# Where the causal mask of an attention unit is set: a product on TensorE, or a select on GpSimd

## The chip, the cores and the metric

One NeuronCore of a Trainium2 chip runs the whole program. The metric is device time in microseconds (us). The engines are called PE (TensorE; PEld is its weight load, which overlaps), DVE (VectorE), ACT (ScalarE), POOL (GpSimd) and SP (SyncE, which issues DMAs). Each works through its own queue in order.

## What is computed

The reference runs a gated linear attention (an mLSTM) over 2 batches, 8 heads, 768 positions and 40 values per head, and feeds its output through two gated feed-forward blocks over 1536 tokens, 320 wide, with 1536 hidden columns.

```python
for t in range(S):
    m_new  = max(f[t] + m, i[t])
    C = exp(f[t] + m - m_new) * C + exp(i[t] - m_new) * outer(v[t], k[t])
    n = exp(f[t] + m - m_new) * n + exp(i[t] - m_new) * k[t]
    y[t] = sigmoid(o[t]) * (C @ q[t]) / max(abs(n . q[t]), 1)
x = silu(xn @ w_gate) * (xn @ w_val) @ w_out        # xn: y, rms-normed
z = sigmoid(x @ w2_gate) * (x @ w2_val) @ w2_out
```

The kernel does not step through t. It cuts the 768 positions into six chunks of 128. Inside a chunk every position s acts on every later t with the weight exp(u[t] + a[s]) times the score k[s].q[t], and nothing acts on an earlier t: that is the causal mask. What came before the chunk is in a state matrix.

## The kernel before

**Units.** A unit is one chunk of one batch: unit u holds chunk u // 2 of batch u % 2, so there are twelve, and units 4 to 11 are chunks two to five (counted from zero). For a unit, `a_bcast_pe` (L270) builds the exponents in two PSUM tiles `A`, each 128 x 512 (s on the partitions, four heads of 128 values of t along a row). Per half it takes: one product of the bf16 identity with `negm` (L259, in `a_bcast0`), which writes 0 where t >= s and -1e30 elsewhere; one product with `picked` (L275), which adds one gate term; and four narrow products (L278), which add the other. `a_exp` (L300) has ACT take the exponential of each half into the SBUF tile `E` (L304), so a masked place becomes 0. `a_scores` (L309) computes the scores into PSUM, eight products per unit and half pair (L317); `a_weigh` (L320) has DVE multiply each half of `E` by its scores in place (L324). `a_out` (L326) uses `E` as weights of the output product (L337), after the product with the state (L333). Normalisation, gating, transposing and splitting follow. `A` and the scores share the two PSUM buffers of tag `sc`; `E` has two SBUF buffers.

**Feed-forward.** `steps` is a list of (block, token group, hidden tile) slots. A slot runs sixteen products into PSUM (`up`, L454), the activation on ACT and DVE (L483 to L486 for the first block), a subtraction on POOL that makes the low part of the hidden tile (L487), and two slots later the down products (L465 to L467). Weights arrive as 544 KB pieces in `wraw` (three buffers, L96) and go through ACT (L100, L107, L120) and DVE (L111, L124) to become a high and a low part. The first token groups run while later attention units are still being computed, so PE has both in one queue.

**What sets the order.** The work of units 0 and 1 is written out by hand. From unit 3 on, each operation has a due time (`want`, L562): a unit starts a set lead ahead of the slot that needs it, its stages stand 1.5 us apart (`stg`), and a planner that estimates each operation places all of them in the queues of the engines. So the queues before are a plan's result, and a changed operation can move others in it. In a unit, the first stage holds `a_scale`, `a_bcast_pe` and `a_exp`, the second `a_scores`, `a_wv` and `a_gate`, the third `a_weigh`, the fourth `a_out`.

**What else POOL does** in that stretch: L487 (hT), L287 (`wv`), L349 (state decay), L407 (`r`), L413 (a copy of `y`).

Of the kernel before, what the change touches and what calls it, by code (L numbers as in the profile page):

```python
# [12 lines left out]
AF = mybir.ActivationFunctionType  # L13
ALU = mybir.AluOpType
# [5 lines left out]
L = 128  # L20
# [22 lines left out]


PE_ADD = 6

G2 = [(0, 2), (2, 4), (6, 4), (10, 2)]
T = dict(
    visits=[(0, 0, 12), (1, 0, 12), (2, 0, 12), (3, 0, 12)],
    start=9.89, d0=4.6, d1=2.84, d2=5.36, w0=1.9, w1=-11.36, wld=9.1, lead=(33, 35, 35, 35, 42, 60), skew=3.0, stg=1.5,  # L50
# [6 lines left out]
def attention_then_two_moe(tc, fi, fir, qk, qt3, nat, w1, w2, rms_g, consts, out):  # L57
    nc = tc.nc
# [9 lines left out]
    def psum(tag):  # L68
        return ps.tile([128, 512], F32, tag=tag, name=tag, bufs=2)
# [9 lines left out]
    rows3 = [ap.tile([KR, 3, L], BF16, name=f"rows3_{b}", bufs=1) for b in range(B)]  # L79
# [150 lines left out]
    def col(u, k):  # L230
        c, b = divmod(u, B)
        if c == 0:
            return col0[:, k * BH + b * H:k * BH + (b + 1) * H]
        o = b * H * NR + c - 1
        return colR[:, o:o + (H - 1) * NR + 1:NR]
# [18 lines left out]
    def a_bcast0(u, tag="up"):  # L254
        d = X.setdefault(u, {})
        d["E"] = ap.tile([128, H, L], F32, tag="E", name="E")
        d["A"] = [psum(tag) for _ in range(2)]
        for hh in range(2):
            nc.tensor.matmul(d["A"][hh], lhsT=identb, rhs=negm.unsqueeze(1).to_broadcast([128, 4, L]), start=True, stop=False)  # L259

    def a_bcast0b(u, hh):
# [5 lines left out]
    def picked(r, n, m):  # L267
        return pick[:, r:r + (n - 1) * NR + 1:NR].unsqueeze(2).to_broadcast([KR, n, m])

    def a_bcast_pe(u):  # L270
        c, b = divmod(u, B)
        a_bcast0(u, "sc")
        for hh in range(2):
            o, r = X[u]["A"][hh], hh * 4 * NR + c - 1
            nc.tensor.matmul(o, lhsT=rows3[b][:, 1], rhs=picked(r, 4, L), start=False, stop=False)  # L275
            for h in range(4):
                one = pick[:, r + h * NR:r + h * NR + 1].to_broadcast([KR, L])
                nc.tensor.matmul(o[:, h * L:(h + 1) * L], lhsT=one, rhs=rows3[b][:, 0], start=False, stop=(h == 3))  # L278
# [21 lines left out]
    def a_exp(u, hs=range(H)):  # L300
        E, A = X[u]["E"], X[u]["A"]
        if u >= B:
            for hh in range(2):
                nc.scalar.activation(E[:, 4 * hh:4 * hh + 4, :].rearrange("p h t -> p (h t)"), A[hh], AF.Exp)  # L304
            return
        for h in hs:
            nc.scalar.activation(E[:, h, :], A[h // 4][:, h % 4 * L:(h % 4 + 1) * L], AF.Exp, bias=col(u, 0)[:, h:h + 1])
# [43 lines left out]
    def a_state(u):  # L351
# [6 lines left out]
        for g in range(NG):  # L358
            n = GW if g < 2 else 2 * E1
            o = s[0:KR, g * GW:g * GW + n]  # L360
            add = B <= u < PE_ADD
            nc.tensor.matmul(o, lhsT=d["nat"][:, g * KR:(g + 1) * KR], rhs=wv[:, g * GW:g * GW + n], start=True, stop=not add)
# [3 lines left out]
    def a_update(u):  # L366
# [4 lines left out]
        st = St[b].rearrange("p g e -> p (g e)")[:, 0:NV]  # L371
        if u < PE_ADD:
            nc.vector.tensor_tensor(out=st, in0=blk, in1=d["C"][0:KR, 0:NV], op=ALU.mult)
# [234 lines left out]
    def unit(u):  # L608
        t = t_unit(u) + (u % B) * T["skew"]
        st = [  # L610
            [a_scale, a_bcast_pe, a_exp] if u > B else [a_scale, a_exp],
            [a_scores, a_wv, a_gate],
            [a_weigh] if u < PE_ADD else [a_weigh, a_state],
            [a_out, a_decay, a_state, a_update] if u < PE_ADD else [a_out, a_decay, a_update],
            [a_norm1, a_norm1b, a_norm1c],
            [a_norm2],
            [a_norm3, a_flip],
            [a_xt],
        ]
        if u >= B:  # L620
            want(t - T["uld"], lambda: a_load(u))
        for k, fns in enumerate(st):
            want(t + k * T["stg"], *[lambda fn=fn: fn(u) for fn in fns])
# [7 lines left out]
    with tc.manual_schedule(engines=set(engines)):  # L631
# [6 lines left out]
        for t, fill in ((ident, 1.0), (identb, 1.0)):  # L638
            nc.gpsimd.memset(t, 0.0)
            nc.gpsimd.affine_select(out=t, in_=t, pattern=[[1, 128]], compare_op=ALU.not_equal,  # L640
                                    fill=fill, base=0, channel_multiplier=-1)
# [5 lines left out]
                                fill=NEG, base=0, channel_multiplier=-1)  # L647
        nc.gpsimd.memset(mhalf, -0.5)
        nc.gpsimd.memset(pick, 0.0)
        for k in range(3):  # L650
            nc.gpsimd.affine_select(out=pick, in_=pick, pattern=[[1, 9 * NR]], compare_op=ALU.not_equal,
                                    fill=1.0, base=k * H * NR, channel_multiplier=-1)
        nc.gpsimd.memset(blk9, 1.0)
        b4 = blk9.rearrange("p (g j e) -> p g j e", g=NG, j=3)
        for base, cm, st in ((0, 1, -D), (D - 1, -1, D)):
            nc.gpsimd.affine_select(out=b4, in_=b4, pattern=[[0, NG], [st, 3], [0, E1]], compare_op=ALU.is_ge,
                                    fill=0.0, base=base, channel_multiplier=cm)
# [10 lines left out]

        keep_warm(wm[0])
        a_bcast0(0)  # L670
        g_first()
        g_max()
# [14 lines left out]
        g_first_a()  # L687
        a_bcast0b(0, 1)
        a_exp(0)
        w_bits(0, 0, 0)  # L690
        a_load(1, (3,))
# [4 lines left out]
        w_hi(0, 0, 0)  # L696
        w_pre(0, 0, 1)
        a_bcast0(1)
        a_bcast0b(1, 0)
        a_bcast0b(1, 1)  # L700
        w_bits(0, 0, 1)
        g_first_ws()
        a_exp(1)
        keep_warm(wm[2])
        w_lo(0, 0, 0)
# [21 lines left out]
        a_norm1b(1)  # L727
        a_norm2(0)
        a_bcast_pe(2)
        a_norm1c(1)  # L730
        a_norm2(1)
# [38 lines left out]
    for s, (moe, g, m, f, l) in enumerate(steps):  # L770
# [6 lines left out]
        r = []  # L777
# [81 lines left out]
```

## Time and profile before

| | us |
|---|---|
| runs | 543.25, 538.78, 543.01 |
| median | 543.01 |
| profiled execution | 540.2 |
| span of its profile (first to last instruction) | 538.5 |
| mean granted clock of TensorE | 0.971 of full speed |

The profile lists busy time by engine, the chain of work that ended last, the costliest groups of instructions and the DMA queues. A busy PE is not PE at its peak, since matmuls are pipelined and their ends are modelled; the start of one matmul to the start of the next is what one costs the queue. The granted clock has two levels, 2.4 GHz (1.00) and 1.2 GHz (0.50); a figure between them is a stretch that holds some of both.

### The profile page before, as it was taken

The numbers are of one execution on the slowest core, as the hardware profiler recorded it, in microseconds if no ns is written. First come the engines' busy times: TensorE is split into PE (matmuls) and PEld (weight loads), VectorE is DVE, ScalarE is ACT, GpSimd is POOL, SyncE is SP. The second block draws the span as 40 slices with busy tenths as digits, with TensorE's granted clock in tenths as the row PEclk, the third lists the DMA queues.
The fourth block names the chain that finished last, engine by engine and source line by source line (L and its number), as shares of the span: only waits on it lengthen the run. The fifth ranks groups of instructions, "written<-read, shape, count | busy, mean of one in ns | idle before, by whom it ended". The sixth has DMA issues, their size and how long they took to land.

```text
span 538.5 us, 9054 instructions
## 1 busy us (share of the span) xinstructions
PE 518.2 (96%) x3592; PEld 478.5 (89%) x3592; DVE 260.1 (48%) x540; ACT 232.4 (43%) x518; POOL 95.2 (18%) x148
## 2 busy tenths in 40 slices
PE   7779999799999999999999999999999999999997
PEld 5668888799999988999999999998888888888996
DVE  5768879444243433654765756643233232323322
ACT  4669878533222322332757666643222222222222
POOL 7112233243223221222321212110000000000000
PEclk9888999799989997999999999999999999999999
DMA  6598878411021112100225333100000010000100
GB/s 187 177 287 271 265 240 257 169 53 40 1 77 53 40 47 71 54 1 1 84 85 167 116 134 120 48 0 13 13 0 2 0 42 8 1 0 1 50 1 25
DMA packets 15752, 43.09 MB, mean 80 GB/s; under 512 B 1822, under 2 KB 6734, under 8 KB 15710
## 3 DMA queue, kind: packets, MB, share of 16 engines
q1 hardware_dynamic: 15518, 42.27, 25.0%
q8 instruction: 28, 0.46, 0.4%
q10 hardware_dynamic: 192, 0.25, 0.1%
q14 instruction: 14, 0.11, 0.1%
HBM read 40.32 MB, written 2.01 MB: 79 GB/s over the span
## 4 chain that ended last, share of the span: by engine, by line
PE 67%; DMA 15%; ACT 8%; DVE 7%; issue 3%; SPq 0%; ACTq 0%; DVEq 0%
PE up L454 29%; DMA wraw<-in_w_dram 12%; PE sc L454 8%; PE dn L465 4%; PE dn L467 4%; PE dn L466 4%; PE at L337 4%; DVE wT L111 3%; PE sc L317 2%; ACT wT L100 2%; ACT wraw L107 2%; PE at L466 2%; PE at L467 2%; PE at L465 2%; ACT wH L120 1%
## 5 line engine op out<-in xcount | busy, mean ns | idle before, releaser
L454 PE MATMUL up<-xT,wH 128*128 128x256 f32 x940 | 166.9, 291 | 2.5 <-DVE th L485 2.5
L454 PEld LDWEIGHTS up<-xT,wH 128*128 128x128 f32 x940 | 137.5, 194 | 5.7 <-DVE th L485 3.9
L454 PE MATMUL up<-xT,wL 128*128 128x256 f32 x564 | 103.3, 289 | 1.1 <-DVE wL L124 1.1
L487 POOL TENSOR_TENSOR hT<-th,hT 128x256 fp32r<-128x256 f32 x72 | 58.7, 815 | 162.5 <-ACT hT L486 122.9
L454 PEld LDWEIGHTS up<-xT,wL 128*128 128x128 f32 x564 | 83.5, 194 | 2.0 <-DVE wL L124 1.6
L484 DVE SCALAR_TENSOR_TENSOR th<-th,up 128x256 f32<-128x256 f32 x72 | 30.0, 417 | 64.4 <-ACT th L483 64.2
L465 PE MATMUL dn<-wH,hT 128*128 128x320 f32 x184 | 58.3, 317 | 0.5 <-ACT hT L486 0.5
L466 PE MATMUL dn<-wL,hT 128*128 128x320 f32 x184 | 57.3, 312 | 0.0
L467 PE MATMUL dn<-wH,hT 128*128 128x320 f32 x184 | 57.1, 317 | 0.0
L538 ACT ACTIVATE th<-up 128x256 f32<-128x256 f32 (+1 forms) x48 | 23.5, 490 | 73.0 <-PE up L454 72.8
L483 ACT ACTIVATE th<-up 128x256 f32<-128x256 f32 x72 | 27.3, 379 | 49.1 <-PE up L454 46.9
L539 DVE SCALAR_TENSOR_TENSOR th<-th,sc 128x512 f32<-128x512 f32 x24 | 16.5, 687 | 64.1 <-PE sc L454 64.0
L540 ACT CAST hT<-th 128x256 fp32r<-128x256 f32 (+1 forms) x48 | 24.6, 513 | 50.0 <-DVE th L539 50.0
L111 DVE SCALAR_TENSOR_TENSOR wT<-wT,wraw 128x544 int32<-128x544 int32 x48 | 36.8, 769 | 17.2 <-ACT wraw L107 9.8
L486 ACT CAST hT<-th 128x256 fp32r<-128x256 f32 x72 | 29.0, 403 | 33.6 <-DVE th L485 33.3
L107 ACT ACTIVATE wraw<-wraw 128x544 int32<-128x544 uint16 x48 | 33.8, 705 | 20.9 <-DMA wraw<-in_w_dram 20.6
L541 DVE TENSOR_TENSOR hT<-th,hT 128x256 fp32r<-128x256 f32 (+1 forms) x48 | 28.0, 583 | 25.0 <-ACT hT L540 24.9
L100 ACT ACTIVATE wT<-wraw 128x544 f32<-128x544 f32 x48 | 33.3, 703 | 11.4 <-DMA wraw<-in_w_dram 11.2
L465 PEld LDWEIGHTS dn<-wH,hT 128*128 128x128 f32 x184 | 35.1, 191 | 1.8 <-ACT hT L486 0.7
L124 DVE TENSOR_TENSOR wL<-wT,wH 128x544 fp32r<-128x544 f32 x46 | 34.1, 767 | 5.1 <-ACT wH L120 4.8
L466 PEld LDWEIGHTS dn<-wL,hT 128*128 128x128 f32 x184 | 35.0, 190 | 0.9
L467 PEld LDWEIGHTS dn<-wH,hT 128*128 128x128 f32 x184 | 34.4, 190 | 0.5
(183 smaller groups left out, 834.8 us busy)
## 6 DMA issues: line engine op xcount, KB each, us to landing
wraw<-in_w_dram SPq DMA_DIRECT2D x48, 544.0 KB, 4.4
qk<-in_qk_dram SPq DMA_DIRECT2D x12, 416.0 KB
nat<-in_nat_dram SPq DMA_DIRECT2D x12, 324.0 KB, 2.9
nat<-in_nat_dram SPq DMA_DIRECT2D x12, 180.0 KB, 6.6
qt<-in_qt_dram SPq DMA_DIRECT2D x10, 180.0 KB
out_dram<-x2n SPq DMA_DIRECT2D x11, 160.0 KB, 1.9
rows<-x2n SPq DMA_DIRECT2D x6, 30.0 KB
gB<-in_rms_g_dram SPq DMA_DIRECT2D x1, 160.0 KB
```

Of the source, the lines that this page charges most:

```text
L100: nc.scalar.activation(t.bitcast(F32), wraw[moe, m, p][:, :, 1].bitcast(F32), AF.Prelu, scale=2.0 ** -112, alpha=2.0 ** 32)
L107: nc.scalar.activation(raw[:, :, 0], top, AF.Copy, scale=2.0 ** -13, bias=2.0 ** -14 - 0.5)
L111: nc.vector.scalar_tensor_tensor(out=t, in0=t, scalar=3, in1=raw[:, :, 0], op0=ALU.logical_shift_left, op1=ALU.bitwise_or)
L124: nc.vector.tensor_tensor(out=wL[moe, m][:, sl], in0=wT.pop((moe, m, p)).bitcast(F32), in1=wH[moe, m][:, sl].bitcast(F32), op=ALU.subtract)
L454: mm = nc.tensor.matmul(o, lhsT=a, rhs=b, start=(n == 0), stop=(n == 7))
L465: nc.tensor.matmul(o, lhsT=hi, rhs=wo[0], start=first, stop=False)
L466: nc.tensor.matmul(o, lhsT=hi, rhs=wo[1], start=False, stop=False)
L467: pe_last[0] = nc.tensor.matmul(o, lhsT=lo, rhs=wo[0], start=False, stop=last)
L484: nc.vector.scalar_tensor_tensor(out=th, in0=th, scalar=1.0, in1=gt, op0=ALU.add, op1=ALU.mult)
L486: nc.scalar.copy(hT[:, 0, :], th)
L487: nc.gpsimd.tensor_tensor(out=hT[:, 1, :], in0=th, in1=hT[:, 0, :].bitcast(F32), op=ALU.subtract)
L541: nc.vector.tensor_tensor(out=hT[:, 1, :], in0=th, in1=hT[:, 0, :].bitcast(F32), op=ALU.subtract)
```

## The change

For units 4 to 11 the two products with `negm` are left out, and the product with `picked` starts the accumulation instead. Each half of `E` is masked in SBUF after the exponential: POOL keeps it where t - s >= 0 and writes 0 elsewhere, in place, with one `affine_select` over 128 x 512. Units 0 to 3 are as they were.

```diff
+LATE = 4
 def a_bcast0(u, tag="up"):
     ...
-    for hh in range(2):
+    for hh in range(2) if u < LATE else ():
         nc.tensor.matmul(d["A"][hh], lhsT=identb, rhs=negm..., start=True, stop=False)
 def a_bcast_pe(u):
     ...
-        nc.tensor.matmul(o, lhsT=rows3[b][:, 1], rhs=picked(r, 4, L), start=False, stop=False)
+        nc.tensor.matmul(o, lhsT=rows3[b][:, 1], rhs=picked(r, 4, L), start=(u >= LATE), stop=False)
 def a_exp(u, hs=range(H)):
     ...
-                nc.scalar.activation(E[:, 4 * hh:4 * hh + 4, :].rearrange("p h t -> p (h t)"), A[hh], AF.Exp)
+                e = E[:, 4 * hh:4 * hh + 4, :]
+                nc.scalar.activation(e.rearrange("p h t -> p (h t)"), A[hh], AF.Exp)
+                if u >= LATE:
+                    nc.gpsimd.affine_select(out=e, in_=e, pattern=[[0, 4], [1, L]], compare_op=ALU.is_ge,
+                                            fill=0.0, base=0, channel_multiplier=-1)
```

## Rows read from the trace of the kernel before

**Rows 1.** The page's busy time by engine: us, share of the span, instructions.
```profile
PE 518.2 (96%) x3592; PEld 478.5 (89%) x3592; DVE 260.1 (48%) x540; ACT 232.4 (43%) x518; POOL 95.2 (18%) x148
```

**Rows 2.** Stretches: length, busy of PE, PEld, DVE, ACT, POOL; clock, DMA share, GB/s.
```profile
36.00:98.40 62.40, 55.99 (x435) 49.59 (x434) 51.10 (x95) 51.09 (x105) 18.05 (x20) 0.97 0.85 268
98.40:256.50 158.10, 158.10 (x1201) 151.28 (x1202) 68.27 (x167) 49.37 (x130) 40.53 (x62) 0.94 0.14 42
256.50:344.00 87.50, 84.76 (x656) 82.76 (x656) 56.24 (x112) 58.10 (x126) 18.85 (x26) 1.00 0.35 116
344.00:538.50 194.50, 190.72 (x1140) 173.14 (x1138) 61.25 (x112) 54.70 (x110) 5.39 (x9) 1.00 0.03 11
```

**Rows 3.** Chain of waits, 36 to 98.4 us: shares by line, then two pieces (start, length).
```profile
by line: DMA wraw<-in_w_dram 40.2%; DMA nat<-in_nat_dram 11.0%; DVE wT L111 10.0%; issue 7.7%; DVE wL L124 7.7%; ACT wT L100 7.2%; ACT wraw L107 6.4%; ACT wH L120 2.8%; DVE th L484 2.4%; DVE th L485 2.0%; DVE y L400 1.7%; DVE E L324 1.6%; A
...
89.79 6.83 DMA nat<-in_nat_dram
...
98.36 1.09 PE at L333 x6
```

**Rows 4.** Chain of waits, 98.4 to 256.5 us: shares by line; then its next piece.
```profile
by line: PE up L454 46.4%; PE at L337 10.5%; PE sc L317 8.4%; PE dn L465 7.2%; PE dn L467 6.7%; PE dn L466 6.6%; PE at L333 3.5%; PE at L362 2.4%; PE sc L259 1.6%; PE sc L278 1.6%; PE sc L275 1.5%; PE at L364 0.8%; PE at L295 0.7%; PE at L4
...
256.51 0.49 ACT xT L424
```

**Rows 5.** L259's group (ns min/median/max); PE in order of time: start, length.
```profile
L259 PE MATMUL sc<-masks x20: 377/390/650, 24.7 to 217.7; 128*128 128x512 bf16 x20
...
151.09 0.39 PE L259 MATMUL sc<-masks 128*128 128x512 bf16 x1
151.31 0.38 PE L275 MATMUL sc<-pick,rows 120*128 120x512 bf16 x1
...
205.52 0.65 PE L259 MATMUL sc<-masks 128*128 128x512 bf16 x1
205.96 0.63 PE L275 MATMUL sc<-pick,rows 120*128 120x512 bf16 x1
```

**Rows 6.** Groups of instructions by form, POOL's selects: busy us, mean ns, idle before.
```profile
L656 POOL TENSOR_SCALAR_AFFINE_SELECT early<-early 120x369 f32<-120x369 f32 x2 | 1.2, 584 | 0.1
L651 POOL TENSOR_SCALAR_AFFINE_SELECT pick<-pick 120x45 bf16<-120x45 bf16 x3 | 0.7, 227 | 0.2
L640 POOL TENSOR_SCALAR_AFFINE_SELECT ident<-ident 128x128 f32<-128x128 f32 x1 | 0.3, 292 | 0.1
```

**Rows 7.** In order of time: unit 4's exponential and weighing; unit 8's weighing and output.
```profile
62.35 0.61 ACT L304 ACTIVATE E<-sc 128x512 f32<-128x512 f32 x1
65.94 0.68 DVE L324 TENSOR_TENSOR E<-E,sc 128x512 f32<-128x512 f32 x1
...
193.70 0.69 DVE L324 TENSOR_TENSOR E<-E,sc 128x512 f32<-128x512 f32 x1 [1.96 <-PE sc L317]
197.77 0.80 PE L337 MATMUL at<-nat,E 128*128 128x41 f32 x6
```

**Rows 8.** POOL's waits, 96 to 258 us: total us, times, longest.
```profile
POOL hT L487 <- ACT hT L486: 36.6, 20, 5.4
```

**Rows 9.** Three lines' groups: ns min/median/max, first and last start.
```profile
L487 POOL TENSOR_TENSOR hT<-th,hT x72: 722/737/1301, 46.8 to 358.7; 128x256 fp32r<-128x256 f32 x72
L124 DVE TENSOR_TENSOR wL<-wT,wH x46: 707/718/1252, 16.0 to 356.2; 128x544 fp32r<-128x544 f32 x46
L324 DVE TENSOR_TENSOR E<-E,sc x24: 672/682/689, 11.7 to 227.9; 128x512 f32<-128x512 f32 x24
```

**Rows 10.** Stretches of 3 us around one fall of the clock; columns as in rows 2.
```profile
153.00:156.00 3.00, 3.00 (x26) 2.80 (x24) 1.56 (x4) 1.19 (x3) 1.52 (x2) 1.00 0.19 61
156.00:159.00 3.00, 3.00 (x17) 2.75 (x17) 1.20 (x3) 0.18 (x1) 0.00 (x0) 0.66 0.21 41
159.00:162.00 3.00, 3.00 (x15) 3.00 (x14) 1.47 (x5) 1.32 (x4) 0.35 (x1) 0.50 0.30 101
162.00:165.00 3.00, 3.00 (x18) 2.55 (x18) 0.62 (x2) 0.38 (x1) 0.18 (x1) 0.71 0.61 172
```

## The prediction

> **What bounds the kernel now.** I read the page's busy times first: PE is at 96%, no other engine reaches 50%, and POOL, which takes the new work, stands at 18% [rows 1]. That is an average over stages, so the second view is the table of stretches, cut where the chain of waits changes hands, and the third is that chain within each stretch. The reader is to see four stages in them. From 36 to 98.4 us PE, DVE and ACT are each busy for 51 to 56 of 62.4 us and the DMA engines are at 0.85 [rows 2]; the chain runs through weight pieces from memory and their conversion on ACT and DVE, no PE line is among its named shares, and it ends in a DMA of `nat` (89.79 to 96.62) on which PE's L333 at 98.36 hangs through ACT and DVE [rows 3]. From 98.4 to 256.5 PE is busy all of the 158.1 us [rows 2] and the chain is PE's own queue, line after line [rows 4]. From 256.5 the chain leaves PE for ACT (L424) [rows 4] and then the weight stream of the second block; from 344 to the end it is PE again. So PE time that is taken out counts fully between 98.4 and 256.5. What follows begins from PE's end there (L424 splits what PE has just transposed), so I let it move along whole.
>
> **What the change removes.** Eight units times two products make 16 instructions of L259 (the line has 20 of this form; units 2 and 3 keep four). One is 390 ns long by its median, but its price is the distance to the next start: 151.09 to 151.31, that is 0.22 us at the 2.4 GHz level, and 205.52 to 205.96, 0.44 us at 1.2 GHz [rows 5]. Six of the sixteen (units 4 to 6) stand at 58 to 92 us, in the stage where PE is not on the chain: 6 x 0.22 = 1.3 us of PE work that I count as nothing, because the DMA and conversion chain covers it; were PE the limit there, they would be worth that 1.3. The ten of units 7 to 11 lie between 151 and 218 us, on the chain. L259 has 1.6% of that stretch's chain [rows 4]: 0.016 x 158.1 = 2.5 us. By instructions it comes to the same: seven at 0.22 and three at half clock or at its edge, between 0.22 and 0.44 each, make 2.2 to 2.9. The 16 weight loads overlap PE's products (PEld is a queue of its own, busy for less than PE [rows 2]) and count as nothing; without that cover they would be at most one load ahead of each product. **Term 1: -2.5 us**, with -3.8 (all sixteen) as the far end.
>
> **What it adds.** Sixteen selects over 128 x 512 on POOL. The trace has none of this shape; the nearest are 128 x 128 at 292 ns, 120 x 369 at 584 ns and 120 x 45 at 227 ns [rows 6]. From 128 to 369 columns a column costs (584 - 292) / 241 = 1.21 ns, so 512 columns take 292 + 384 x 1.21 = 757 ns. The lower end takes the slope from 45 to 128 columns, 65 / 83 = 0.78 ns: 0.59 us. The upper end takes what POOL's own work is stretched by when DVE is busy, 1301 against 722 ns [rows 9]: 0.76 x 1.8 = 1.37 us. I take 0.76, nearest to the measured select of 369 columns. Sixteen make 12 us on an engine that is busy for 40.5 of 158 us in the stretch where it matters [rows 2], so POOL stays far from being a bound.
>
> **What it puts in series.** `a_weigh` now waits for the select. What hides it is the gap that already stands between exponential and weighing, because the scores have to come through the same two PSUM buffers after the exponential. Unit 4 has the smallest gap that I found: its exponential ends at 62.96 and the weighing starts at 65.94, 3.0 us [rows 7]; the other gaps read for units 4 to 11 run from 3.2 us upward. A free POOL needs 0.76, a stretched one 1.37. The scores do not wait for the select, since it works on `E` in SBUF and the exponential has released `A`. Behind the weighing there is more cover: unit 8's second half is weighed by 194.39, and its output product starts at 197.77, 3.4 us later [rows 7]. If the cover were gone, queued behind the weighing on DVE are L484 and L485, which release the `up` buffers, and so PE. The POOL queue behind a waiting select holds L487, whose result the down products need two slots later. **Term 2: 0 us**; without cover 0.76 per half, 10 x 0.76 = 7.6 us in the PE stage.
>
> **What POOL does to DVE.** L324, which reads one tile of SBUF and one of PSUM, always took 672 to 689 ns. L124, with two inputs in SBUF, took 707 to 1252, and POOL's L487 722 to 1301 [rows 9]: the two engines hold each other up when both have two SBUF inputs. In the first stage L111 and L124 are on the chain [rows 3], and four selects (units 4 and 5) fall there. A select that meets such an instruction may cost DVE up to 1252 - 707 = 0.55 us, so 0 to 2.2 us. A select has one input where those POOL instructions have two, and DVE is in other work part of the time; I take **Term 3: +0.5 us**. After 98.4 DVE has room (68 of 158 us [rows 2]) and the same contention is free. The Trainium skill, "GPSIMD Engine Reference", section 1 (Specifications), says that GpSimd shares its SBUF interfaces with VectorE and that they contend where a DVE instruction runs in a two-port mode or has two SBUF inputs. The trace agrees, with 689 ns as the longest L324 and 1252 as the longest L124; by that rule alone each of the four selects would meet an L111 or L124, and the sum would lose the gain down to 0.3 us.
>
> **The sum.** -2.5 + 0 + 0.5 = -2.0 us, bounds of the parts -3.8 and -0.3. The profiled execution took 540.2 us (span 538.5 and 1.7 around it), so it would take 538.2. That execution is 2.8 below the median of 543.01, and the runs themselves lie 4.5 apart. The four executions have a mean of (543.25 + 538.78 + 543.01 + 540.2) / 4 = 541.3, and I set the forecast against that: **539.3 us**.
>
> **Rivals.** (a) **One half-clock stretch fewer.** Three times between 96 and 210 us PE fell to 1.2 GHz. The fall at 157 has 2.0 + 3.0 + 1.7 = 6.8 us at half clock (from the shares 0.66, 0.50 and 0.71) [rows 10], and so cost 3.4 us; the others, at 99 and 202, look alike in the same view. With one less: -2.0 - 3.4 = -5.4, 535.9 us. For it: other PE work closes up where the products stood. Against it: nothing in the change reaches the wait for `nat` before the first one.
> (b) **One more.** In the stretch ahead of the second fall PE was busy for all 3.00 us, with 26 products, many of them narrow ones of attention (40 rows or 41 columns), and the clock fell without an idle gap [rows 10]. The change takes two 512-column products out of each unit and leaves the narrow ones, which speaks for a further fall: -2.0 + 3.4 = +1.4, 542.7 us. The Trainium skill, "TensorE: Matmul & The Clock Gate", section "Why this matters for your kernels", ties such falls to idle gaps of PE; the trace differs here, busy 3.00 of 3.00 us ahead of the fall, and by the page the clock would stay as it is.
> (c) **Slower: a select stuck in POOL's queue.** POOL works in order and waits for its next hT 20 times for 36.6 us in this stage, 1.8 us on average and 5.4 at the longest [rows 8]. A select planned behind such an L487 makes the weighing late from the point where wait plus 0.76 passes the gap of 3.0 us, that is from 2.2 us. At the longest wait: 5.4 + 0.76 - 3.0 = 3.2 us on DVE, handed to PE, and an idle PE may lose a stretch of clock too: 3.2 + 3.4 - 2.0 = +4.6, 545.9 us for one, over 550 for two. Against it: hT and the exponential both follow PE's progress, and POOL has been idle for three quarters of the stage [rows 2].
> (d) **Nothing comes of it.** The planner places everything anew, the weight stream at 256 us starts where it did, and PE only waits longer there: 541.3.
>
> **Chances.** Forecast 0.48, (a) 0.17, (b) 0.14, (c) 0.13, (d) 0.08. The predicted time is the forecast's. Its own range, from the bounds of the parts and the spread of the runs, is 536 to 543. The range asked for reaches down through (a), set against the profiled execution (534.8), and up through one case of (c): 534.5 to 546.0; a double (c) and two stretches of clock fewer are left out. About 1% (5.4 us) is what a measurement of this kernel can tell from no change. Faster by more: half of (a) and the far end of the forecast, 0.23. Slower by more: the heavier part of (c) and a little of (b), 0.11. Within 1%: 0.66.
>
> **What would show it.** In the profile after: four L259 of this form instead of 20 and 16 selects near 0.76 us, longer ones before 98 us (term 2's price); the idle time of DVE before L324 still put down to the scores and not to POOL (term 2); L111 and L124 no longer than before, up to 0.55 us where a select overlaps them (term 3); PE's stretch from L333's wait to the hand-over to the second block shorter by 2.5 us (term 1). Three half-clock stretches again decide between the forecast and (a) or (b). The prediction is wrong if PE shows new waits in 98 to 256 us, or if the plan moved a load or a unit as a whole.

## The result, and the profile after

The changed kernel took 524.47 us (median; 523.57 to 528.35), the kernel before beside it 543.13 (538.78 to 547.26). The ratio is 0.9687, with a 95% interval of 0.9638 to 0.9736: faster by 3.1%. The prediction of 539.3 us and its range from 534.5 were wrong; the time lies 10 us below the range. Ratios here leave out disturbed runs (in `short` and `both` seven of ten), medians and means are over all runs, so they need not agree.

Of the profile after (execution 524.49 us, span 522.7), the busy times, the granted clock over the span in 40 slices (tenths) and the shares of the chain of waits, with the last line once more from the page before:

```profile
PE 503.7 (96%) x3576; PEld 466.8 (89%) x3576; DVE 260.4 (50%) x540; ACT 232.0 (44%) x518; POOL 105.3 (20%) x164
...
PEclk9769979999999999999999999999999999999999
...
PE 76%; DMA 10%; ACT 6%; DVE 5%; issue 2%; SPq 0%; ACTq 0%; DVEq 0%
```
```profile
PE 67%; DMA 15%; ACT 8%; DVE 7%; issue 3%; SPq 0%; ACTq 0%; DVEq 0%
```

Against [rows 1], PE lost 14.5 us of busy time with 16 products fewer, POOL gained 10.1 with 16 instructions more, DVE and ACT stayed. The products left out cannot be 14.5 us: sixteen of the longest, 0.65 us [rows 5], would be 10.4. PE's share of the chain rose, that of the DMAs fell. The clock tells one part: before, the same line of the page was

```profile
PEclk9888999799989997999999999999999999999999
```

with dips in slices 8, 12 and 16, the falls near 99, 157 and 201 us. After, nothing dips behind the sixth slice; ahead of it the dips are deeper than before (7, 6 and 7 in slices 2, 3 and 6, against 8, 8 and 9).

**Where the time went.** The first stages end at no common moment, so I cut both kernels at the same work: the first and the 48th POOL instruction that makes hT. Between them lie 217.1 us before and 199.6 after (columns as in [rows 2]).

```profile
46.79:263.87 217.08, 211.73 (x1614) 199.42 (x1614) 118.83 (x263) 97.19 (x231) 58.93 (x83) 0.95 0.31 95
```
```profile
46.85:246.48 199.63, 195.82 (x1599) 187.29 (x1599) 119.31 (x263) 97.16 (x231) 68.66 (x97) 0.98 0.34 107
```

All of the gain is made here: the stretch is 17.4 us shorter, 1.6 more than the whole span (538.5 against 522.7). PE's instructions are fewer by 15, and DVE and ACT are busy for about as long as before. Sharing out PE's time by the distance from one product's start to the next, with idle time and what the half clock adds booked by themselves, gives:

| between the two marks, us | before | after | difference |
|---|---|---|---|
| products with `negm` | 3.6 | 0 | -3.6 |
| score products | 18.3 | 13.8 | -4.4 |
| lost to the half clock | 10.2 | 3.4 | -6.8 |
| output, state and transposes | 34.0 | 33.0 | -1.0 |
| idle | 5.3 | 3.8 | -1.5 |
| the other products of the exponent | 6.9 | 7.1 | +0.2 |
| up and down | 138.6 | 138.4 | -0.3 |

Four fifths of the gain stand on lines that the diff does not touch. The gain comes in steps, at the three places where the clock fell before: hT by hT the changed kernel is ahead by 4 to 5 us between 116 and 155 us (by the trace of before), by 9 to 10 between 166 and 197, by 15 at 211, and by 16 to 18 from 222 on. The sequence of PE's work shows why: the planner laid out the queues anew. Unit 6's output and unit 7's scores before and after (start, length):

```profile
153.01 0.79 PE L333 MATMUL at<-St,qt 120*128 120x123 f32 x6
153.64 1.02 PE L337 MATMUL at<-nat,E 128*128 128x41 f32 x8
154.59 1.16 PE L317 MATMUL sc<-qk 40*128 40x128 f32 x8
155.68 0.41 PE L337 MATMUL at<-nat,E 128*128 128x41 f32 x2
156.02 1.26 PE L317 MATMUL sc<-qk 40*128 40x128 f32 x8
157.21 1.50 PE L337 MATMUL at<-nat,E 128*128 128x41 f32 x6
158.51 0.61 PE L465 MATMUL dn<-wH,hT 128*128 128x320 f32 x1
```
```profile
147.76 0.79 PE L339 MATMUL at<-St,qt 120*128 120x123 f32 x6
148.39 1.47 PE L343 MATMUL at<-nat,E 128*128 128x41 f32 x12
149.79 1.17 PE L323 MATMUL sc<-qk 40*128 40x128 f32 x16
150.89 0.64 PE L343 MATMUL at<-nat,E 128*128 128x41 f32 x4
151.36 0.39 PE L471 MATMUL dn<-wH,hT 128*128 128x320 f32 x1
```

(A score product is two instructions.) Before, the two halves' scores stand apart: 8 instructions from 154.59 to 155.68 (1.09 us) and 8 from 156.02 to 157.21 (1.19). After, all 16 stand together with the halves in turns, and take 1.10 us (149.79 to 150.89). Half 0 reads partitions 0 to 39 and half 1 partitions 64 to 103, and in the trace the two run side by side: after, instructions start in pairs 13 to 14 ns apart, the next pair 98 to 99 ns later; before, within a half, one starts 111 to 112 ns behind the other. Before, the stretch in which PE does only narrow products of attention is 5.5 us long and ends at half clock [rows 10]; after, it is 3.6 us and the clock stays:

```profile
147.00:150.00 3.00, 3.00 (x29) 2.94 (x29) 1.13 (x3) 1.81 (x4) 2.32 (x5) 1.00 0.10 30
150.00:153.00 3.00, 3.00 (x32) 2.88 (x31) 2.08 (x6) 1.05 (x3) 0.79 (x1) 1.00 0.38 105
```

The fall at 99 went with the idle time ahead of it. Before, PE idled for 2.7 us ahead of L333, with 0.64 us busy out of 3.00 at 96 to 99, then ran at 0.50. After, the same operation waits for 0.68 us and starts at 94.86 [rows 3: 98.36], and PE goes on at full clock. PE's wait, then the stretches, before and after:

```profile
PE at L333 <- DVE qt L298: 2.7, 1, 2.7
...
96.00:99.00 3.00, 0.64 (x5) 0.64 (x6) 1.87 (x5) 1.58 (x4) 0.72 (x1) 0.99 1.00 382
99.00:102.00 3.00, 3.00 (x17) 3.00 (x16) 0.72 (x2) 1.51 (x4) 1.49 (x2) 0.50 0.47 167
```
```profile
PE at L339 <- DVE qt L300: 0.7, 1, 0.7
...
93.00:96.00 3.00, 2.32 (x22) 2.09 (x20) 3.00 (x6) 1.97 (x4) 0.89 (x2) 1.00 1.02 296
96.00:99.00 3.00, 3.00 (x27) 3.00 (x27) 1.96 (x5) 1.57 (x3) 1.48 (x2) 1.00 0.99 336
```

The planner moved loads too, and this wait goes with them. Before, SyncE issues the load of `nat` [rows 3: 89.79] behind one of `qk`; after, it stands at 87.06 ahead of that load and of two weight pieces, and ACT reads `nat` at 91.57 instead of 96.64. In all, 6 of the 117 transfers in SyncE's queue stand elsewhere.

The table books two half-clock stretches less, not three: after has one of 6.8 us at 66, in the stage bound by the weights, behind 2.1 us in which PE waited.

### The profile page after: what moved, and what is told of

It reads as the page before. It is cut to its first block, busy times and chain, and to the rows that moved or that the text cites. A ratio compares the mean times of both kernels' runs of the same rounds, so it can differ in the third digit from the quotient of the medians.

```text
span 522.7 us, 9043 instructions
## 1 busy us (share of the span) xinstructions
PE 503.7 (96%) x3576; PEld 466.8 (89%) x3576; DVE 260.4 (50%) x540; ACT 232.0 (44%) x518; POOL 105.3 (20%) x164
## 4 chain that ended last, share of the span: by engine, by line
PE 76%; DMA 10%; ACT 6%; DVE 5%; issue 2%; SPq 0%; ACTq 0%; DVEq 0%
PE up L460 34%; DMA wraw<-in_w_dram 9%; PE sc L460 9%; PE dn L471 5%; PE dn L473 5%; PE dn L472 5%; PE at L343 4%; PE sc L323 2%; DVE wT L113 2%; PE at L471 2%; PE at L472 2%; PE at L473 2%; ACT wT L102 2%; ACT wH L122 2%; ACT wraw L109 1%
## 5 line engine op out<-in xcount | busy, mean ns | idle before, releaser
L460 PEld LDWEIGHTS up<-xT,wH 128*128 128x128 f32 x940 | 136.0, 192 | 7.5 <-DVE th L491 5.4
L460 PE MATMUL up<-xT,wL 128*128 128x256 f32 x564 | 101.2, 287 | 0.3 <-DVE wL L126 0.3
L460 PEld LDWEIGHTS up<-xT,wL 128*128 128x128 f32 x564 | 82.3, 192 | 0.7 <-DVE wL L126 0.5
L126 DVE TENSOR_TENSOR wL<-wT,wH 128x544 fp32r<-128x544 f32 x46 | 34.2, 770 | 7.1 <-ACT wH L122 6.9
```

Source lines behind the costliest of these rows:

```text
L126: nc.vector.tensor_tensor(out=wL[moe, m][:, sl], in0=wT.pop((moe, m, p)).bitcast(F32), in1=wH[moe, m][:, sl].bitcast(F32), op=ALU.subtract)
L460: mm = nc.tensor.matmul(o, lhsT=a, rhs=b, start=(n == 0), stop=(n == 7))
```

## The experiments

Theory: the gain comes from the order of the queues, which the planner changed when two instructions left its list; the diff's own parts are worth what the prediction gave them. First rival: the products cost far more than their 0.22 us each. Second rival: the selects, which put a wait between exponential and weighing, bring the gain. "Pairs" below counts neighbouring score products, in the order of PE's queue, that belong to different halves; half-clock stretches are those of the one profiled execution that begin between 90 and 500 us.

| kernel | median us | ratio to before | interval | pairs | half clock, from us |
|---|---|---|---|---|---|
| before | 543.1 | 1 | | 17 | 98.9, 156.9, 201.3 |
| after | 524.47 | 0.9687 | 0.9638 to 0.9736 | 39 | none |
| long | 525.59 | 0.9646 | 0.9585 to 0.9707 | 39 | none |
| short | 543.79 | 0.9876 | 0.9809 to 0.9944 | 17 | 100.7, 158.7, 199.7 |
| both | 542.45 | 0.9895 | 0.9804 to 0.9986 | 17 | 99.0, 157.0 |
| none | 526.15 | 0.9664 | 0.9561 to 0.9768 | 41 | none |
| b_stg14 | 526.84 | 0.9731 | 0.9665 to 0.9797 | 40 | none |
| unpair | 527.74 | 0.9704 | 0.9634 to 0.9774 | 16 | none |
| thin | 532.76 | 0.9828 | 0.9744 to 0.9912 | 39 | 192.9 |
| dense | 540.17 | 0.9961 | 0.9908 to 1.0013 | 17 | 102.1 |
| b_stg16 | 542.05 | 0.9983 | 0.9942 to 1.0025 | 18 | 101.3, 166.1, 207.1 |
| a_stg14 | 523.76 | 0.9662 | 0.9612 to 0.9711 | 32 | none |
| a_stg17 | 528.62 | 0.9724 | 0.967 to 0.9779 | 35 | none |

### The products put back into the new order (long)

The queues are those of the changed kernel; behind each product with `picked` of units 4 to 11 one product with `negm` and its weight load are put in after the planner is done. The selects stay.

```diff
 # in a_bcast_pe, units 4 to 11: the picked product's name is kept in FIRSTS
+for blk in nc.m.functions[0].blocks:          # after planning
+    new = []
+    for i in blk.instructions:
+        new.append(i)
+        if i.name in FIRSTS:                  # same PSUM tile, adds negm
+            new += [copy_of(load_of_identb), copy_of(i, ins=negm_product.ins, start_tensor_calc=False)]
```

> The changed kernel's queues as they are, with the sixteen negm products put back on TensorE, each behind the product with picked of its half (the selects stay, so a place is masked twice). Theory 'order': the products are worth what they take, 16 x 0.22 = 3.6 us in PE time, and the other 13 to 15 us come from another order of TensorE's queue. Then this takes 524.5 + 3 to 4 = 528 us, with the score products still 16 in 1.1 us and no half-clock stretch between 100 and 260 us. Theory 'products': leaving the products out is itself what gains (they cost more than their starts show, or they bring the falls of the clock). Then this is back at 538 to 543 us.

525.59 us against 524.47 of the changed kernel; the means of both are 525.2. In the profile the products of the exponent take 10.7 us instead of 7.1 between the two marks, so the 16 cost 3.5 of their own. What the whole run pays for them, the scatter of the runs does not tell from nothing. The rival that they are dear falls: with all of them in place the kernel keeps the gain.

### The products made short in the old order (short)

The queues are those of the kernel before; the products of units 4 to 11 write 4 of 512 columns, so the mask inside these chunks is left out, and nothing else moves.

```diff
+if i.name in NEGS:      # after planning, units 4 to 11
+    new[k] = dataclasses.replace(i, outs=[4 columns], ins=[4 columns, ...], stop_tensor_calc=True)
+elif i.name in FIRSTS:  # the picked product starts the sum
+    new[k] = dataclasses.replace(i, start_tensor_calc=True)
```

> The kernel before with its own queues, the negm products of units 4 to 11 cut to 4 of 512 columns after planning; the causal mask inside those chunks is left out. Theory 'order': 543 - 2.5 to 3.5 = 540 us, with the three half-clock stretches and the half-by-half scores (8 in 1.1 us) of before. Theory 'products': about 525 us, as the changed kernel.

543.79 us by the median, 0.3 under before beside it; 1.1 by the mean of all ten; 1.2% by the ratio (0.6 to 1.9%), which rests on three of the ten. All three half-clock stretches are there, and the scores stand as before. In the old order the products are worth between 3 and 10 us by the interval and next to nothing by the median; the 18.7 are out of its reach. With `long` it says: the order carries most of the gain, the products little.

### Products and selects together (both)

The kernel before, and the selects on POOL for units 4 to 11 as in the change; the planner lays it out.

```diff
 nc.scalar.activation(e..., A[hh], AF.Exp)
+if u >= LATE:
+    nc.gpsimd.affine_select(out=e, in_=e, ..., compare_op=ALU.is_ge, fill=0.0, ...)
```

> Products and selects both, planned anew. Theory 'order': the planner gets the same TensorE work as before, so its order should be like that of before, and so should the time, 543 us within 4. A rival that the select itself brings the gain (by holding the weighing back, so that both halves of the scores stand together): about 528 us.

542.45 us, ratio 0.9895 (0.9804 to 0.9986). The order of PE's queue came out as that of before, product by product, and SyncE's too. The selects show no cost and do not bring the gain. The spread of its runs, 534.12 to 547.39, goes with the clock (below).

### Neither product nor select (none)

The changed kernel without the selects, so the mask in chunks two to five is left out.

```diff
-if u >= LATE:
-    nc.gpsimd.affine_select(out=e, in_=e, ..., compare_op=ALU.is_ge, fill=0.0, ...)
```

> The changed kernel without its selects (no mask inside chunks two to five, so the output is not causal there): products left out, nothing added on GpSimd. Theory 'order': TensorE's queue has the score products in turns as in the changed kernel, and the selects are hidden, so 524 us, within 2 of the changed kernel. A rival that the selects cost time which the changed kernel pays: below 522 us.

526.15 us; 0.9664, where the changed kernel has 0.9687. The order of PE is that of the changed kernel but for some up products and one block of scores. The select shows no cost in this place, and the second rival falls.

### Another spacing of the stages, and nothing of the mask changed (b_stg14)

The kernel before, with one number of the planner's table changed.

```diff
-    ... skew=3.0, stg=1.5,
+    ... skew=3.0, stg=1.4,
```

> The kernel before, every instruction of it, with the stages of a unit 1.4 us apart in the due times instead of 1.5: another order out of the same planner. In its TensorE queue the score products of the two halves stand in turns 40 times (17 before, 39 in the changed kernel) and the longest stretches of attention products without feed-forward products between them are shorter than before. Theory 'order': 525 to 531 us, with nothing of the mask changed. Theory 'products' (a gain only where products are left out): 538 to 546 us.

526.84 us, ratio 0.9731. All products with `negm` and no select are in it, and it has the gain but for 2.4 us, by the medians. Its PE works on the same two units as the changed kernel does, with all 16 score instructions in 1.09 us:

```profile
151.71 0.79 PE L333 MATMUL at<-St,qt 120*128 120x123 f32 x6
152.34 1.92 PE L337 MATMUL at<-nat,E 128*128 128x41 f32 x16
154.19 1.16 PE L317 MATMUL sc<-qk 40*128 40x128 f32 x16
155.28 0.41 PE L465 MATMUL dn<-wH,hT 128*128 128x320 f32 x1
```

This decides: an order is enough, whatever is done with the mask. (Its profiled execution had a half-clock stretch of 13.7 us at 81.7, ahead of those that the table lists.)

### Scores half after half in the new order (unpair)

The queues of the changed kernel; where score products stand next to each other, half 0's come first, then half 1's.

```diff
+run = the neighbouring score products in PE's queue       # after planning
+for place, i in zip(places, sorted(run, key=lambda i: (half(i), head(i)))):
+    queue[place] = i       # names and waits stay with the place
```

> The changed kernel's queues, but inside each run of neighbouring score products the four heads of one half go first and then the four of the other, not in turns. If products of the two halves run side by side when they alternate (they start at partitions 0 and 64), this costs what the traces differ by: about 4.6 us between the same two slots, so 529 us; and if long stretches of narrow products bring the clock down, one or two half-clock stretches of 3.4 us come back, up to 536 us. If the alternation is of no account: 524.5 us.

527.74 us, 3.3 more than the changed kernel by the median, with intervals that overlap for the most part. The block at unit 7 now takes 1.64 us (151.57 to 153.21), where in turns it took 1.10:

```profile
151.57 1.71 PE L324 MATMUL sc<-qk 40*128 40x128 f32 x16
153.21 0.64 PE L345 MATMUL at<-nat,E 128*128 128x41 f32 x4
```

Four blocks between the marks changed in this way, and the scores there rose from 13.8 to 15.7 us. The stretches grew (3.6 to 4.1 us at unit 7), but no half-clock stretch came back in the profiled execution. It is the quickest of the four, at a mean clock of 0.984; the others had 0.968 to 0.974, and where theirs fell no trace shows. So the turns are worth some 1.9 us of PE's time in this trace; what of it reaches the end, the scatter does not tell, since by the means 2.6 of the 3.2 us go with the clock. That is less than the -4.4 of the table: standing together, 16 instructions take 1.64 us even half after half, where the two blocks of 8 before took 1.09 and 1.19.

### Wide products between the narrow ones (dense)

The queues of before; in units 6 and 8 one bf16 product with 328 columns that adds zero goes behind each of seven output products, 14 in all.

```diff
+    new.append(i)                       # after planning
+    if i.name in OUTS:                  # output products of units 6 and 8, heads 0 to 6
+        new += [copy_of(load_of_identb), zero_product(328 columns, same PSUM tile)]
```

> The kernel before in its own order, with seven extra wide products (328 columns of zeros, added to the output tile, value unchanged) between the eight output products of unit 6 and of unit 8, the two stretches after which the clock fell at 157 and 201 us. They add 14 x 0.14 = 2 us. Theory 'narrow stretches bring the clock down': the falls at 157 and 201 go or get rarer, the mean granted clock rises from 0.960 to about 0.975, and the time falls by 2 x 3.4 - 2 = 4 to 5 us, to 539 us. If the falls have to do with how long attention products run without feed-forward products, whatever their width: clock as before and 546 us.

540.17 us, ratio 0.9961 (0.9908 to 1.0013). In the profiled execution the falls at 157 and 201 are gone, though nothing is moved and the added products take 2.5 us of their own (one of 13.7 us at 64.6 is there instead). Some of them in order of time, then the table of stretches, and the last stretch in before:

```profile
157.03 0.31 PE L260 MATMUL at<-masks 128*128 128x328 bf16 x1
157.18 0.31 PE L339 MATMUL at<-nat,E 128*128 128x41 f32 x2
```
```profile
159.00:162.00 3.00, 3.00 (x25) 2.59 (x24) 1.38 (x2) 0.18 (x1) 0.20 (x1) 1.00 0.14 20
...
201.00:204.00 3.00, 3.00 (x24) 2.71 (x25) 1.74 (x5) 0.18 (x1) 0.00 (x0) 1.00 0.00 0
```
```profile
201.00:204.00 3.00, 3.00 (x14) 2.73 (x14) 1.75 (x5) 0.18 (x1) 0.00 (x0) 0.55 0.00 0
```

Against before, the stretch 159 to 162 has 25 instructions at 1.00 where [rows 10] has 15 at 0.50, and 201 to 204 has 24 where before had 14 at 0.55. The fall at 102, behind the wait for `nat`, stays. The mean clock over all its runs is 0.971, before 0.962: on average less was won back than in the profile, and the interval of the time includes no change. So the run goes with the theory that the narrow products bring down the clock in these two places, but does not show it: `both`, with PE's queue of before and no wide product added, had no fall at 201 either, and only 3.4 us of one at 157. What the traces do show is that PE was busy for all of the time, with a fall and without.

### More narrow products in the new order (thin)

The queues of the changed kernel; six of eight score products of units 7 and 9 are taken three times, with the same result; each copy stands by its original, so the halves are in turns only in part there.

```diff
+    new.append(i)                        # after planning
+    if i.name in SCORES and not i.has_update():
+        new += [copy_of(i), copy_of(i)]
```

> The changed kernel in its own order, with the score products of units 7 and 9 taken three times (the same values written again), which lengthens the two stretches of attention products at 148 and 186 us from 3.6 and 4.1 us to about 6. By their own time the 24 extra instructions cost 3 to 5 us: 528 us. Theory 'narrow stretches bring the clock down': one or two half-clock stretches appear behind them, 3.4 us each, 531 to 536 us, clock down by 0.007 to 0.014 from 0.979. If the falls have another cause: 528 us at an unchanged clock.

532.76 us. The products themselves added 5.0 us; one half-clock stretch of 6.8 us (3.4 lost) appeared at 192.9, with PE busy throughout (the order of time, then the stretches):

```profile
188.99 4.73 PE L325 MATMUL sc<-qk 40*128 40x128 f32 x40
193.65 1.07 PE L347 MATMUL at<-nat,E 128*128 128x41 f32 x4
```
```profile
189.00:192.00 3.00, 3.00 (x31) 3.00 (x31) 0.91 (x2) 0.00 (x0) 0.59 (x1) 1.00 0.13 46
192.00:195.00 3.00, 3.00 (x19) 2.78 (x18) 1.00 (x3) 0.18 (x1) 0.00 (x0) 0.65 0.14 19
```

The other lengthened stretch, 5.9 us at 146.5, had no fall, and the mean clock over the runs stayed at 0.979. So the theory of the clock is borne out in one place of two; the length of a stretch alone does not decide it (`b_stg16` had 4.1 us of narrow products at 161.7 with a fall behind them, the changed kernel 4.1 at 185.9 without one).

### More spacings (b_stg16, a_stg14, a_stg17)

The kernel before with `stg` 1.6, the changed kernel with 1.4 and 1.7, edits as in `b_stg14`. They ask whether the new order belongs to the change or is one that the planner falls into.

> The kernel before with stages 1.6 us apart: the same instructions as before in a third order. Its TensorE queue looks like that of before: the score products of the two halves in turns 18 times (17 before), long attention stretches at the same two places. Theory 'order': 540 to 546 us, as before. If a shift of the stages gains by itself, or every other order is better than that of before by chance: 525 to 530 us.

> The changed kernel with stages 1.4 us apart. Score products in turns 32 times (39 at 1.5), attention stretches no longer than 4 us. Theory 'order': within 3 us of the changed kernel, 522 to 528 us. If the changed kernel's order is a rare one: 535 us or more.

> The changed kernel with stages 1.7 us apart. Score products in turns 35 times, fewest long attention stretches of the orders looked at. Theory 'order': 521 to 527 us, clock at or above 0.979. If the changed kernel's order is a rare one: 535 us or more.

542.05, 523.76 and 528.62 us. With the products in the plan, spacings of 1.5 and 1.6 give the slow order (17 and 18 pairs) and 1.4 the fast one; without them 1.4, 1.5 and 1.7 all give a fast one (32, 39 and 35 pairs). `a_stg17` came out 1.6 us above what was expected. The loads divide the kernels in the same way as the pairs of the planned orders: with a slow order (before, `short`, `both`, `dense`, `b_stg16`) SyncE's queue is that of before, and each trace has a wait of 1.9 to 5.4 us for `qt` ahead of a fall between 98 and 103 us; with a fast one 6 to 9 transfers stand elsewhere, and no trace has that fall. No run moved the loads alone. `a_stg14` is 0.7 us under the changed kernel, less than the runs scatter. No version here is measurably faster than the changed kernel.

## Why the prediction was wrong

**The step that failed is the one that has no term.** The sum adds what the edit takes from and gives to the queues of before, keeps every other instruction in its place, and lets what follows "move along whole". But the queues are a plan, and they were planned anew. The text knew it ("the plan moved a load or a unit as a whole" would make it wrong, and both were moved; rival (d) has the planner place everything anew) and gave it no size but (d)'s, a gain of nothing. `long` has the products and `none` lacks the selects, and both keep the new order and the gain; `b_stg14` has neither part of the change and makes 16 us by order alone. The rest of the steps:

**Term 1 (products, -2.5, far end -3.8): right in size.** Four products of the form are left, and the sixteen cost 3.6 us in before's trace between the marks and 3.5 in `long`. What of that reaches the end, `long` (1.1 by the median, 0 by the mean) and `short` (0.3 by the median, 1.1 by the mean, 3 to 10 by the ratio) leave open.

**Term 2 (select in series, 0): right.** Two lines' groups after (ns min/median/max, first and last start), then two waits (total us, times, longest):

```profile
L309 POOL TENSOR_SCALAR_AFFINE_SELECT E<-E x16: 629/638/1220, 64.0 to 206.1; 128x512 f32<-128x512 f32 x16
L126 DVE TENSOR_TENSOR wL<-wT,wH x46: 705/720/1250, 15.4 to 340.1; 128x544 fp32r<-128x544 f32 x46
```
```profile
POOL E L309 <- ACT E L307: 13.3, 8, 8.1
DVE E L330 <- PE sc L323: 5.8, 4, 2.5
```

A select took 638 ns by the median and 1220 at most (estimate 757, ends 590 and 1370). The least time between a select's end and its weighing was 1.2 us, in unit 4 (65.14 to 66.36), where the prediction's gap of 3.0 less 0.76 would leave 2.2; the cover held. POOL waits for the exponential, and the weighing's idle time is put down to the scores, as the prediction said, never to POOL. Rival (c), a select stuck in POOL's queue, did not occur.

**Term 3 (contention on DVE, +0.5): nothing seen.** The low-part line, L126 above, took 705, 720 and 1250 ns, as before [rows 9: 707, 718, 1252]; DVE's busy time rose by 0.3 us over the whole kernel.

**Rival (a), a half-clock stretch fewer, had the right sign and the wrong reach.** It took one, for 3.4 us. Between the marks two fewer were booked, 6.8 us. By the mean over the runs, span times the clock missing, 20.8 us were lost before (45 runs) and 10.9 after (4): at most some 10 of the 18.7 us. Among the 45, a us more of clock missing went with only 0.5 us more of time, so less than that may reach the end. Its argument against itself, that nothing reaches the wait for `nat`, fell with the order: that wait shrank from 2.7 to 0.68 us.

**Rival (b) had the wrong sign, and its mechanism is not shown.** It held that narrow products alone bring the clock down; `dense` and one place of `thin` go with this, `both` does not. It then reckoned with the same stretches, less their wide products. In the new order the stretches themselves were 3.0 to 4.1 us instead of 5.5 to 7.2. The Trainium skill, "TensorE: Matmul & The Clock Gate", section "Why this matters for your kernels", ties such falls to idle gaps: the fall at 99 is of that kind (0.64 of 3.00 us busy ahead of it), those at 157 and 201 and the one of `thin` are not (PE busy 3.00 of 3.00).

**Missing altogether: the scores.** No step asked what neighbours a product has. The trace of before had the price in it: 8 instructions of one half in 1.09 us.

What stays open: why the plan tips between spacings of 1.4 and 1.5 with the products in it and not without them, what the moved loads are worth without the moved products, what brings down the clock under a busy PE, and how the gain shares out between clock, scores, idle time and products over many runs; the table shares it for one execution.

## What to carry to other kernels

Where a planner makes the order, an edit has two effects: its own, and that of a new plan. Measure the second by itself: keep the old order and edit the instructions after planning, and leave the code alone and nudge one number of the planner; when a nudge moves the time by more than the edit's own sum, the planner's numbers are what to tune. In the trace, read what stands beside what on PE before summing durations.

## What the runs showed of the hardware

**Score products of 40 rows run side by side when their halves lie on different partitions and stand in turns.** Sixteen instructions took 1.10 us in turns, 1.64 half after half, and 1.09 plus 1.19 in two blocks with other work between; in turns the two halves' instructions started 13 to 14 ns apart. The Trainium skill, "TensorE: Matmul & The Clock Gate", section "The mechanism" of Part 3, says that products on different row groups overlap while all start and end in the order of the program. The trace agrees: it is the order in the queue that made 1.64 out of 1.10.

**The clock fell under a fully busy PE,** behind stretches of narrow products only (156.9 and 201.3 before, 192.9 in `thin`), and in one execution with wide products put between, that of `dense`, the two falls of before were not there; nor was that at 201 in `both`, which has no such products. A stretch's length did not settle it: 4.1 us fell in `b_stg16`, 4.1 in the changed kernel and 5.9 in `thin` did not.

**The same program differs from run to run with its clock.** Runs of the kernel before lay between 537.0 and 550.0 us; one of 537.85 had a mean granted clock of 0.974, one of 547.76 had 0.945. A difference of a few us in such a kernel is first to be looked for in the mean granted clock.
